# Fewer, longer turns between scoring and weighing in a fused attention and feed-forward kernel

## The chip, the core and the metric

The kernel runs on one core of one Trainium2 chip. The metric is the device time of one execution in microseconds (us); lower is better. Before the change it is 1427.97 us, the median of three runs that lie between 1427.86 and 1428.01 us. Engines are called PE (matrix multiply; PEld are its weight loads), ACT (activation), DVE (vector), POOL (GpSimd) and SP (SyncE, which here issues most of the DMA transfers).

## The reference

The reference is one transformer block without masks, in float32: 2048 tokens, width 512, 32 query heads of width 16 that share one key and one value head, and a gated feed-forward part of width 1792.

```python
q = heads(ln(x) @ wq); k = ln(x) @ wk; v = ln(x) @ wv     # 32 heads of 16; one k, one v
p = softmax(q @ k.T / 4, axis=-1)
h = x + merge(p @ v) @ wo
g = ln(h)
out = h + (gelu(g @ w_gate) * (g @ w_up)) @ w_down
```

## The kernel before

**Blocks and groups.** The queries are cut into four blocks of 512 tokens (NB = 4), the heads into eight groups of four (NG = 8), and the keys into sixteen chunks of 128 (KC = 16). For one group and one block, `score` (L952) is called 32 times, twice for each key chunk. One call is a **pair**: two heads of the group against one chunk. `scores` (L357) runs a pair as two matmuls (L364) on the upper and lower 64 rows of PE at the same time, into one of two PSUM tiles of two banks, and then one exponential of 128x1024 on ACT (L368) into half of a tile `p`. The next pair but one uses the same PSUM tile again, so its matmuls wait until that exponential is done.

**Weighing.** When a chunk's two pairs are through ACT, `weigh` (L370) multiplies `p` with the values, in four matmuls on four column strips of PE (L372), eight in the trace because float32 takes two passes. The sums of a group gather in one bank, `acc`. After the sixteenth chunk `evacuate` (L383) copies `acc` on DVE (L385), sends it to DRAM and fetches it back in another layout (L386, L396), all on SP's queue.

**Cycles.** Scoring uses PE in halves of 64 rows, weighing in strips of 32 columns. The program collects several pairs and then weighs what is finished: that is a **cycle**. `SIZES` (L978) says how many pairs the six cycles of a group have: 6, 5, 5, 6, 5, 5. `finish` (L929) weighs every chunk whose second pair is older than the newest call; at the last cycle of a group (L1093) it weighs all that is left. In a six-cycle group the numbers of weighed chunks are 2, 3, 2, 3, 3, 3.

**Dense work between the pairs.** While attention runs on one block of queries, PE also does the projection and the feed-forward part of the block before (`dense`, L560). That work comes as a generator of **steps**, where one step is two matmuls on the two halves of 64 rows. In the woven part (`weave`, L823) two jobs of twelve steps run side by side, one on each half, and each job changes halves in the middle. After each pair the loop at L1040 draws as many steps as a table of shares says. `WOVEN` (L1030) gives a 6-pair cycle (0, 5, 3, 3, 3, 0), so none after its first pair, five after the second, three after the third, fourth and fifth, and none after the last. A 5-pair cycle gets (0, 5, 3, 3, 0), the last of a group (0, 5, 4, 3, 0) from `LAST` (L1031). That is 73 steps a group. `kinds` (L1032) lays a block's run of dense work over the cycles: four "long" ones and a "gap" for the projection and normalisation, 36 "woven" ones, then four "long" and two "short" ones, which have tables of their own (L1024, L1025). With LEAD (L980) this puts the woven part of each of three blocks from within group 1 to within group 7, and groups 2 to 6 are woven all through.

**Weights.** The gate and up weights of a block are 28 tiles of 512 KB (tile 2f is the gate, 2f + 1 the up part of slice f), in four buffers. `load_w1` (L510) is called for tile i + 4 when the job of tile i is done (L713), so each load stands at that place of SP's queue, and waits there until PE has freed the buffer. Also on SP's queue are the evacuations named above, the next group's queries (`load_q`, L345, two transfers of 200 KB, called at the fifth pair of a group) and the down weights (`load_w2`, L516, 1 MB each). PE, ACT, SP and DVE run these instructions in the order in which the program writes them.

**Gates.** When a gate and an up job are done, DVE and ACT form the gelu. The DVE operations are drawn one after each pair (L1066), and the tanh on ACT (L735) is put at the end of a cycle (`open_gates`, L940) or ahead of the first down job.

Of the kernel before, what the change touches and what calls it, by code (L numbers as in the profile page):

```python
# [48 lines left out]
def kernel(  # L49
# [21 lines left out]
    NB = S // T  # L71
# [3 lines left out]
    NG = H // 4  # L75
    KC = S // P
# [66 lines left out]
    def attend(first):  # L143
        with ExitStack() as outer:
            with tc.manual_schedule(
                engines={mybir.EngineType.PE, mybir.EngineType.Pool, mybir.EngineType.Activation}
            ):
                run(outer, first)


    def run(outer, first):
# [218 lines left out]
        def weigh(acc, p, kc):  # L370
            for j in range(4):
                nc.tensor.matmul(  # L372
                    acc[32 * j : 32 * j + 32, :], v_sb[:, kc, :], p[:, j, :],
                    start=(kc == 0), stop=(kc == KC - 1), skip_group_check=True,
                )
# [3 lines left out]
        def take_out():  # L379
            for step in outs.pop(0):  # L380
                step()
# [541 lines left out]
        PER = NG * KC  # L923
# [3 lines left out]
        pend = []  # L927

        def finish(n):  # L929
            for _ in range(min(n, len(pend))):  # L930
                pb, pg, pkc, pp, pacc, _ = pend.pop(0)
                weigh(pacc, pp, pkc)
                if pkc == KC - 1:
                    evacuate(pb, pg, pacc)
# [5 lines left out]
        def open_gates():  # L940
            while gates:
                gates.pop(0)()
# [9 lines left out]
        def score(n):  # L952

            nonlocal acc
            i, u = divmod(n, 2)
            b, r = divmod(i, PER)
            g, kc = divmod(r, KC)
            if u == 0:
                if kc == 0:
                    cur["qg"] = qgs.pop((b, g))  # L960
                    acc = pss.tile([P, T], F32, tag="acc", bufs=1, name=f"acc_{b}_{g}")
                if kc == 2 and b * NG + g + 1 < NB * NG:
                    key = divmod(b * NG + g + 1, NG)
                    qgs[key] = load_q(*key)
                cur["p"] = sb.tile([P, 4, T], F32, tag="p", bufs=PB, name=f"p_{i}")
            scores(i, cur["p"], cur["qg"], kc, u)
            if u == 1:
                pend.append((b, g, kc, cur["p"], acc, n))
# [6 lines left out]
        width = 1  # L975


        SIZES = (6, 5, 5, 6, 5, 5)  # L978

        LEAD = (3, 2, 2)  # L980
        n, lead = 0, 2 * PER + sum(SIZES[: LEAD[0]])
        with tc.manual_schedule(engines={mybir.EngineType.SP, mybir.EngineType.DVE}):
            parts, said = None, 3
            if first:
# [35 lines left out]
        set_banks("ps_rest")  # L1020
        width = 3

        PLAIN = {5: (0,) * 5, 6: (0,) * 6}
        LONG = {5: (0, 5, 4, 3, 0), 6: (0, 5, 3, 3, 1, 0)}  # L1024
        SHORT = {5: (0, 6, 3, 3, 0), 6: (0, 6, 3, 3, 0, 0)}  # L1025
        assert sum(SIZES) == 2 * KC
        assert [f for fs in RUNS for f in fs] == list(range(FC))
        assert [len(fs) for fs in RUNS] == [4] * (len(RUNS) - 1) + [2]

        WOVEN = {6: (0, 5, 3, 3, 3, 0), 5: (0, 5, 3, 3, 0)}  # L1030
        LAST = (0, 5, 4, 3, 0)  # L1031
        kinds = (  # L1032
            ["long"] * 4 + ["gap"] + ["woven"] * 6 * len(SIZES) + ["long"] * 4 + ["short"] * 2
        )
        todo = list(kinds)
        fixed = ExitStack()
        fixed.enter_context(
            tc.manual_schedule(engines={mybir.EngineType.SP, mybir.EngineType.DVE})
        )
        for c in range(LEAD[0], (NB - 1) * NG * len(SIZES)):  # L1040
            b, cb = divmod(c, NG * len(SIZES))
            if first and (b, cb) in BOUND_STEPS:
                bound_flag(BOUND_STEPS.index((b, cb)))
            cg = cb % len(SIZES)
            size, kind = SIZES[cg], None
            if b > 0 and cb == LEAD[b]:
                assert work is None
                work, todo = dense(b), list(kinds)
            if work is not None:
                kind = todo.pop(0)  # L1050
            if kind == "long":
                shares = LONG[size]
            elif kind == "woven":
                shares = LAST if cg == len(SIZES) - 1 else WOVEN[size]
            elif kind == "short":
                shares = SHORT[size]
            else:
                shares = PLAIN[size]
            due, said = 0, None
            if kind != "woven":  # L1060
                while lazy:
                    lazy.pop(0)()
            for j, share in enumerate(shares):
                score(n)
                n += 1
                if soon or lazy:  # L1066
                    (soon or lazy).pop(0)()  # L1067

                if b > 0 and cb == 1 and j == 3 and outs:
                    take_out()  # L1070

                if kind in (None, "gap") and n % 2 == 0:
                    finish(sum(e[5] < n - 1 for e in pend))
                if kind == "gap" and j == 1:

                    said = next(work)
                due += share
                while due > 0:
                    said = next(work)
                    if said > 0:  # L1080
                        due -= 1
                    elif said == CUT and kind != "short":
                        break

            ends = kind not in (None, "woven") or kind == "woven" and todo[0] != "woven"
            while ends and said not in (CUT, GAP):
                said = next(work)
                assert said < 0, said
            open_gates()
            if work is not None and not todo:  # L1090
                assert next(work, None) is None
                work = None
            finish(sum(e[5] < n - 1 for e in pend) if cg < len(SIZES) - 1 else len(pend))  # L1093
            while behind:
                behind.pop(0)()
            if outs and kind == "woven":
                lazy.extend(outs.pop(0))
            elif outs:
                take_out()
# [261 lines left out]
    def bound_flag(step):  # L1361
        if step == 0:
            nc.gpsimd.dma_start(b2, b_d)
            return
        nc.vector.tensor_reduce(b1, b2, axis=AX.X, op=ALU.max)

        nc.vector.tensor_scalar(flag, b1, (BOUND_MAX / SCALE) ** 2, None, op0=ALU.is_le)
# [69 lines left out]
```

## Time and profile before

| what | value |
|---|---|
| time, median of three runs | 1427.97 us (1427.86 to 1428.01) |
| profiled execution, its own time | 1427.32 us |
| its span, first to last instruction | 1425.5 us |
| granted PE clock, mean | 0.999 |
| instructions in the trace | 25062 |
| mean DMA rate over the span | 127 GB/s |

The profile is one execution. A timeline row gives start and length in us, the engine, the line of the kernel, the operation, output<-inputs by the names in the program, the shape, the number of instructions that the row joins, and in brackets how long the engine had been idle and what ended that. Matmuls overlap, so on PE the distance from one start to the next is what counts, and the length of a row is longer than its share of the time. Rows of SP are the moments of issue of transfers, not the transfers. The windows view gives, for a stretch of time, its length, the busy time and number of instructions of PE, PEld, DVE, ACT and POOL, the granted clock, the busy share of the DMA engines and the rate in GB/s.

### The profile page before, as it was taken

The page shows a single profiled execution, that of the slowest core. Times are in us where ns is not written, and L with a number is a line of the kernel's source. Part 1 is how long each engine was busy: PE and PEld are TensorE (multiplying, and loading weights), DVE is VectorE, ACT ScalarE, POOL GpSimd, SP SyncE. Part 2 cuts the span into 40 slices and gives each one's busy share as a digit, 9 for nine tenths or more (in the row PEclk, how much of TensorE's full clock was granted, in tenths as well). Part 3 has the DMA queues.
Part 4 walks back from the last instruction along what each step waited for, and adds up shares of the span by engine and source line. Part 5 has one row for each costly group of instructions (what it writes and reads, how often), then busy time and mean ns, then how long its engine had stood idle before and what let it go on. Part 6 is the DMA issues. An engine that isn't in the chain of part 4 may idle for free.

```text
span 1425.5 us, 25062 instructions
## 1 busy us (share of the span) xinstructions
PE 1401.7 (98%) x10420; PEld 755.2 (53%) x10420; DVE 544.8 (38%) x985; ACT 1034.3 (73%) x1145; POOL 218.8 (15%) x301
## 2 busy tenths in 40 slices
PE   6999999999999999999999999999999999999998
PEld 5533333224555555555555555554555555557886
DVE  7421322203352433424252432514353342427665
ACT  6699999997777787776877777877777777772000
POOL 5566776731000000000000000000000000000000
PEclk9999999999999999999999999999999999999999
DMA  4456766643242242213252332203343241433551
GB/s 157 145 189 213 230 223 214 214 136 111 83 152 86 93 139 86 86 42 111 94 172 74 102 129 85 87 24 122 101 131 115 87 145 47 138 125 132 176 208 62
DMA packets 66929, 180.56 MB, mean 127 GB/s; under 512 B 9436, under 2 KB 9436, under 8 KB 66776
## 3 DMA queue, kind: packets, MB, share of 16 engines
q1 hardware_dynamic: 56976, 144.79, 30.5%
q0 software_dynamic: 9760, 34.08, 7.3%
q8 instruction: 84, 1.38, 0.4%
q14 instruction: 37, 0.30, 0.1%
q10 hardware_dynamic: 72, 0.00, 0.0%
HBM read 131.13 MB, written 47.71 MB: 125 GB/s over the span
## 4 chain that ended last, share of the span: by engine, by line
PE 91%; ACT 6%; DVE 1%; issue 1%; DMA 0%; SPq 0%; POOL 0%; ACTq 0%; DVEq 0%
PE acc L372 31%; PE s L364 20%; PE pu L858 9%; PE pg L858 7%; ACT p L368 5%; PE pd L858 5%; PE pq L190 4%; PE pd L533 3%; PE pg L555 3%; PE pd L555 3%; PE pu L555 3%; PE pp L533 2%; PE pk L1224 1%; PE pxt L608 1%; PE pt L1214 0%
## 5 line engine op out<-in xcount | busy, mean ns | idle before, releaser
L368 ACT ACTIVATE p<-s 128x1024 f32<-128x1024 f32 x1024 | 965.2, 1059 | 243.1 <-PE s L364 242.4
L372 PE MATMUL acc<-p,v_sb 128*32 128x512 f32 x4096 | 488.2, 598 | 0.1
L364 PE MATMUL s<-qg,kaug 50*128 50x512 f32 x1984 | 395.7, 432 | 4.1 <-ACT p L368 3.3
L364 PEld LDWEIGHTS s<-qg,kaug 50*128 50x128 f32 x1984 | 172.3, 184 | 283.9 <-ACT p L368 164.9
L372 PEld LDWEIGHTS acc<-p,v_sb 128*32 128x32 f32 x4096 | 109.3, 109 | 234.3 <-issue 226.0
L858 PE MATMUL pu<-x2h,w 64*128 64x512 f32 x672 | 211.7, 392 | 0.2 <-DVE g L732 0.2
L858 PE MATMUL pg<-x2h,w 64*128 64x512 f32 x672 | 211.6, 391 | 0.0
L126 POOL TENSOR_SCALAR rstd<-mv 128x1 f32<-128x1 f32 x16 | 3.5, 219 | 984.1 <-DVE mv L124 983.8
L858 PEld LDWEIGHTS pu<-x2h,w 64*128 64x128 f32 x672 | 116.0, 186 | 12.9 <-DVE g L732 0.6
L858 PE MATMUL pg<-x2l,w 64*128 64x512 f32 x336 | 122.6, 392 | 0.0
L858 PEld LDWEIGHTS pg<-x2h,w 64*128 64x128 f32 x672 | 116.3, 186 | 11.1 <-DVE g L732 0.2
L858 PE MATMUL pu<-x2l,w 64*128 64x512 f32 x336 | 122.2, 391 | 0.0
L735 ACT ACTIVATE ga<-ga 128x512 f32<-128x512 f32 x56 | 36.4, 655 | 88.7 <-DVE ga L730 88.7
L858 PE MATMUL pd<-w,gh 64*128 64x512 f32 x384 | 81.4, 391 | 0.0
L385 DVE COPY oT<-acc 128x512 f32<-128x512 f32 x32 | 22.1, 692 | 142.6 <-PE acc L372 142.4
L800 DVE TENSOR_TENSOR h<-h,pd 128x512 f32<-128x512 f32 x48 | 31.9, 685 | 114.5 <-PE pd L858 65.6
L1067 DVE SCALAR_TENSOR_TENSOR ga<-ga,g 128x512 f32<-128x512 f32 x72 | 49.7, 691 | 48.6 <-ACT ga L735 47.1
L401 DVE RECIPROCAL oc<-oc 128x128 f32<-128x128 f32 x64 | 56.3, 922 | 28.8 <-DMA oc<-acc_d 23.7
L719 DVE COPY g<-pg 128x512 f32<-128x512 f32 x56 | 38.7, 692 | 65.8 <-PE pg L858 60.1
L858 PEld LDWEIGHTS pu<-x2l,w 64*128 64x128 f32 x336 | 58.0, 186 | 6.7
L858 PEld LDWEIGHTS pg<-x2l,w 64*128 64x128 f32 x336 | 58.1, 186 | 5.0
L732 DVE TENSOR_TENSOR g<-g,pu 128x512 f32<-128x512 f32 x56 | 38.2, 683 | 40.5 <-PE pu L858 30.2
(251 smaller groups left out, 1387.8 us busy)
## 6 DMA issues: line engine op xcount, KB each, us to landing
w<-w_d SPq DMA_DIRECT2D x112, 512.0 KB
w<-w_d SPq DMA_DIRECT2D x28, 1024.0 KB
qg<-q_d SPq DMA_DIRECT2D x62, 200.0 KB
q_d<-qh SPq DMA_DIRECT2D x32, 256.0 KB
acc_d<-oT SPq DMA_DIRECT2D x32, 256.0 KB
oc<-acc_d SPq DMA_DIRECT2D x128, 64.0 KB
w_d<-w_0b POOLq DMA_DIRECT2D x14, 512.0 KB, 6.6
w_d<-w_1b POOLq DMA_DIRECT2D x14, 512.0 KB, 4.0
```

Of the source, the lines that this page charges most:

```text
L190: nc.tensor.matmul(pq, wt[:, d, c * P : (c + 1) * P], xt[:, d, :], start=(n == 0), stop=(n == 3 * DC - 1),)
L364: nc.tensor.matmul(s[:, a, :], kaug[rows, kc * P : (kc + 1) * P], qg[rows, u, :], start=True, stop=True,)
L368: nc.scalar.activation(p[:, 2 * u : 2 * u + 2, :], s, AF.Exp, scale=SCALE)
L372: nc.tensor.matmul(acc[32 * j : 32 * j + 32, :], v_sb[:, kc, :], p[:, j, :], start=(kc == 0), stop=(kc == KC - 1), skip_group_check=True,)
L401: nc.vector.reciprocal(oc[:, 1, sl], oc[:, 1, sl])
L533: nc.tensor.matmul(banks[k], lhsT[rows], rhs[rows], start=(turn == 0 and i == 0), stop=(turn == 1 and i == n - 1), skip_group_check=True,)
L555: nc.tensor.matmul(bank, lhsT, rhs, start=(i == 0), stop=(i == len(ts) - 1))
L719: nc.vector.tensor_copy(g, pg)
L732: nc.vector.tensor_tensor(g, g, pu, op=ALU.mult)
L735: nc.scalar.activation(a, a, AF.Tanh, scale=GELU_A * GELU_C)
L858: nc.tensor.matmul(e["bank"], lhsT[rows], rhs[rows], start=i == 0 and not e["both"], stop=last and e["both"], skip_group_check=True,)
L1067: (soon or lazy).pop(0)()
```

## The change

Groups 2 to 6 take five cycles of 7, 6, 6, 7 and 6 pairs in place of six. Groups 0, 1 and 7 keep the old sizes. The shares change with them: a 7-pair cycle gets 17 steps, a 6-pair cycle of such a group 13, with two steps in place of three ahead of its last pair. That makes 73 steps a group again, and the chunks weighed in the five cycles are 3, 3, 3, 3 and 4. A block has 43 cycles in place of 48, over three blocks 15 cycles fewer, and the list of kinds has 31 woven entries in place of 36. No matmul, no exponential and no transfer is added or taken away; their order changes.

```diff
-        SIZES = (6, 5, 5, 6, 5, 5)
+        SIXES, FIVES = (6, 5, 5, 6, 5, 5), (7, 6, 6, 7, 6)
+        GROUPS = (SIXES,) * 2 + (FIVES,) * (NG - 3) + (SIXES,)
+        CYCLES = [(g, j) for g in range(NG) for j in range(len(GROUPS[g]))]
...
-        WOVEN = {6: (0, 5, 3, 3, 3, 0), 5: (0, 5, 3, 3, 0)}
-        LAST = (0, 5, 4, 3, 0)
-        kinds = (
-            ["long"] * 4 + ["gap"] + ["woven"] * 6 * len(SIZES) + ["long"] * 4 + ["short"] * 2
-        )
+        WOVEN = {
+            SIXES: {6: (0, 5, 3, 3, 3, 0), 5: (0, 5, 3, 3, 0)},
+            FIVES: {7: (0, 5, 3, 3, 3, 3, 0), 6: (0, 5, 3, 3, 2, 0)},
+        }
+        LAST = {SIXES: (0, 5, 4, 3, 0), FIVES: (0, 5, 3, 3, 2, 0)}
+        woven = len(SIXES) + len(FIVES) * (NG - 3)
+        kinds = ["long"] * 4 + ["gap"] + ["woven"] * woven + ["long"] * 4 + ["short"] * 2
...
-        for c in range(LEAD[0], (NB - 1) * NG * len(SIZES)):
-            b, cb = divmod(c, NG * len(SIZES))
+        for c in range(LEAD[0], (NB - 1) * len(CYCLES)):
+            b, cb = divmod(c, len(CYCLES))
+            group, cg = CYCLES[cb]
+            sizes = GROUPS[group]
...
-            cg = cb % len(SIZES)
-            size, kind = SIZES[cg], None
+            size, kind = sizes[cg], None
...
-                shares = LAST if cg == len(SIZES) - 1 else WOVEN[size]
+                shares = LAST[sizes] if cg == len(sizes) - 1 else WOVEN[sizes][size]
...
-            finish(sum(e[5] < n - 1 for e in pend) if cg < len(SIZES) - 1 else len(pend))
+            finish(sum(e[5] < n - 1 for e in pend) if cg < len(sizes) - 1 else len(pend))
```

More of the change, by code (lines that the diff above doesn't have):

```diff
@@ L975, in run @@
         width = 1
-        SIZES = (6, 5, 5, 6, 5, 5)
+        SIXES, FIVES = (6, 5, 5, 6, 5, 5), (7, 6, 6, 7, 6)
+        GROUPS = (SIXES,) * 2 + (FIVES,) * (NG - 3) + (SIXES,)
+        CYCLES = [(g, j) for g in range(NG) for j in range(len(GROUPS[g]))]
         LEAD = (3, 2, 2)
-        n, lead = 0, 2 * PER + sum(SIZES[: LEAD[0]])
+        n, lead = 0, 2 * PER + sum(SIXES[: LEAD[0]])
         with tc.manual_schedule(engines={mybir.EngineType.SP, mybir.EngineType.DVE}):
@@ L1021, in run @@
         width = 3
-        PLAIN = {5: (0,) * 5, 6: (0,) * 6}
+        PLAIN = {5: (0,) * 5, 6: (0,) * 6, 7: (0,) * 7}
         LONG = {5: (0, 5, 4, 3, 0), 6: (0, 5, 3, 3, 1, 0)}
         SHORT = {5: (0, 6, 3, 3, 0), 6: (0, 6, 3, 3, 0, 0)}
-        assert sum(SIZES) == 2 * KC
+        assert all(sum(sizes) == 2 * KC for sizes in GROUPS)
         assert [f for fs in RUNS for f in fs] == list(range(FC))
         assert [len(fs) for fs in RUNS] == [4] * (len(RUNS) - 1) + [2]
-        WOVEN = {6: (0, 5, 3, 3, 3, 0), 5: (0, 5, 3, 3, 0)}
-        LAST = (0, 5, 4, 3, 0)
-        kinds = (
-            ["long"] * 4 + ["gap"] + ["woven"] * 6 * len(SIZES) + ["long"] * 4 + ["short"] * 2
-        )
+        WOVEN = {
[5 more added lines that the diff above has]
+        kinds = ["long"] * 4 + ["gap"] + ["woven"] * woven + ["long"] * 4 + ["short"] * 2
         todo = list(kinds)
```

## The prediction

> **What bounds the kernel now.** I read the page's busy table first, then its chain of work that ended last, then the timeline of TensorE (PE) for one group of heads whose cycles are all woven, and last the same timeline around two places where cycles were longer than their likes.
>
> ```profile
> PE 1401.7 (98%) x10420; PEld 755.2 (53%) x10420; DVE 544.8 (38%) x985; ACT 1034.3 (73%) x1145; POOL 218.8 (15%) x301
> ...
> PE 91%; ACT 6%; DVE 1%; issue 1%; DMA 0%; SPq 0%; POOL 0%; ACTq 0%; DVEq 0%
> PE acc L372 31%; PE s L364 20%; PE pu L858 9%; PE pg L858 7%; ACT p L368 5%; PE pd L858 5%; PE pq L190 4%; PE pd L533 3%; PE pg L555 3%; PE pd L555 3%; PE pu L555 3%; PE pp L533 2%; PE pk L1224 1%; PE pxt L608 1%; PE pt L1214 0%
> ```
>
> PE carries 91% of the chain, so a change pays only by what it takes from PE's time line. The change leaves every matmul in place: a woven group keeps 32 score pairs, 16 weighings and 73 dense steps. Only the number of turns between scoring and weighing, and what stands between them, can move the time. A cycle starts at the row of four score matmuls, so the differences of these starts are cycle lengths:
>
> ```profile
> 428.43 0.74 PE L364 MATMUL s<-qg,kaug 50*128 50x512 f32 x4
> ...
> 435.21 0.73 PE L364 MATMUL s<-qg,kaug 50*128 50x512 f32 x4
> ...
> 441.91 0.74 PE L364 MATMUL s<-qg,kaug 50*128 50x512 f32 x4
> ...
> 444.57 0.40 PE L364 MATMUL s<-qg,kaug 50*128 50x512 f32 x2
> ...
> 447.69 0.73 PE L364 MATMUL s<-qg,kaug 50*128 50x512 f32 x4
> ...
> 455.32 0.73 PE L364 MATMUL s<-qg,kaug 50*128 50x512 f32 x4
> ...
> 462.00 0.73 PE L364 MATMUL s<-qg,kaug 50*128 50x512 f32 x4
> ...
> 468.87 0.74 PE L364 MATMUL s<-qg,kaug 50*128 50x512 f32 x4
> ```
>
> The six cycles (6, 5, 5, 6, 5, 5 pairs) last 6.78, 6.70, 5.78, 7.63, 6.68 and 6.87 us, 40.44 us together. By the code they weigh 2, 3, 2, 3, 3 and 3 key chunks. The fourth (6 pairs, 14 steps) and the fifth (5 pairs, 11 steps) weigh alike and differ by 0.95 us for a pair and three steps: a pair or a step costs about 0.233 us.
>
> **The change, part by part.** *Cycles.* I price each new cycle from an old one with the same parity of its first pair. Another timeline row gives the price of a weighing, and shows where ScalarE's exponential (ACT) ends the wait:
>
> ```profile
> 608.31 1.92 PE L372 MATMUL acc<-p,v_sb 128*32 128x512 f32 x16
> 610.16 0.73 PE L364 MATMUL s<-qg,kaug 50*128 50x512 f32 x4
> ...
> 614.59 0.49 PE L364 MATMUL s<-qg,kaug 50*128 50x512 f32 x2 [0.15 <-ACT p L368]
> 615.01 2.78 PE L372 MATMUL acc<-p,v_sb 128*32 128x512 f32 x24
> 617.72 0.74 PE L364 MATMUL s<-qg,kaug 50*128 50x512 f32 x4
> ```
>
> Sixteen against 24 matmuls, two against three chunks, are 1.92 against 2.78 us: 0.86 us a chunk. The new group, without waits:
> - first (7 pairs, 17 steps, 3 chunks): 6.78 + 0.93 (a pair, three steps) + 0.86 = 8.57;
> - second and third (6 pairs, 13 steps, 3 chunks): 5.78 + 0.86 + 0.70 (a pair, two steps) = 7.34 each;
> - fourth (7, 17, 3): 5.78 + 0.86 + 2 x 0.93 = 8.50;
> - fifth (6, 13, 4): 6.68 + 0.86 + 0.70 = 8.24.
>
> Sum 39.99, or 0.45 us less than 40.44: the price of one pair of turns.
>
> *What ACT takes back.* The long cycle at 610.16 has 6 pairs, 12 steps, 3 chunks, one step before its last pair, and lasts 7.56 us. The woven 6-pair cycle (7.63 us) less two steps would be 7.16. So the last pair there waits 0.40 us for the exponential that frees its score bank, as the row at 614.59 names. The new 6-pair cycles leave two steps at that place where the old had three. The moment ACT frees the bank stays, so the wait is 0.40 - 0.23 = 0.17 us, three times a group: 0.51. A 7-pair cycle keeps three steps there, and ACT does not fall behind further on:
>
> ```profile
> 448.29 5.61 ACT L368 ACTIVATE p<-s 128x1024 f32<-128x1024 f32 x6 [0.64 <-PE s L364]
> ```
>
> Six of about 1.05 us in 5.61 us start 0.91 us apart, against 0.93 for PE's pair and three steps. Net per group: 39.99 + 0.51 - 40.44 = +0.06, and for 15 groups **+0.9 us**. Bounds: if that wait is nothing, -6.8; if each is the full 0.40, +11. I keep 0.17, since the row beside it differs by one step only.
>
> *Weight loads.* By the instruction order of both kernels, SP issues the same loads; what shifts is how soon after its issue a tile is first used. Two stretches matter, at the start of group 2 in the second and third woven blocks, where the evacuation of the group before holds SP:
>
> ```profile
> 718.80 1.21 SPq L513 DMA_DIRECT2D w<-w_d  x1
> 720.05 0.76 SPq L349 DMA_DIRECT2D qg<-q_d  x2
> 720.86 2.21 SPq L513 DMA_DIRECT2D w<-w_d  x2
> ...
> 1043.67 0.37 SPq L513 DMA_DIRECT2D w<-w_d  x1
> 1044.09 0.76 SPq L349 DMA_DIRECT2D qg<-q_d  x2
> 1044.89 3.12 SPq L513 DMA_DIRECT2D w<-w_d  x2
> ```
>
> The first load is tile 7 (of 28), then come the queries of the next group, then tile 8. What PE did:
>
> ```profile
> 714.02 0.74 PE L364 MATMUL s<-qg,kaug 50*128 50x512 f32 x4
> ...
> 720.80 0.73 PE L364 MATMUL s<-qg,kaug 50*128 50x512 f32 x4
> ...
> 723.14 0.47 PE L858 MATMUL pu<-x2h,w 64*128 64x512 f32 x1
> ...
> 727.88 0.73 PE L364 MATMUL s<-qg,kaug 50*128 50x512 f32 x4
> 728.45 0.39 PE L858 MATMUL pg<-x2h,w 64*128 64x512 f32 x1
> ...
> 1038.91 0.73 PE L364 MATMUL s<-qg,kaug 50*128 50x512 f32 x4
> ...
> 1045.74 0.73 PE L364 MATMUL s<-qg,kaug 50*128 50x512 f32 x4
> ...
> 1048.38 0.47 PE L858 MATMUL pu<-x2h,w 64*128 64x512 f32 x1 [0.23 <-DVE g L732]
> ...
> 1053.12 0.73 PE L364 MATMUL s<-qg,kaug 50*128 50x512 f32 x4
> ```
>
> These second cycles last 7.08 and 7.38 us against 6.70 for their like: PE waited 0.38 and 0.68 us for tile 7, used 4.34 and 4.71 us after its issue. (The view names DVE at 1048.38; the twin at 723.14 has no such release, so I take the load.) In the changed kernel tile 7 is first used at the third step of the second cycle, about 8.57 + 0.57 + 2 x 0.23 = 9.6 us after the group's start; it was there after 9.12 and 9.47. Both waits go: -1.06 us.
>
> Tile 8, used before in the first step of the third cycle (at 728.45, 0.57 us in, and likewise after 1053.12) without a wait, is now used right behind the fourth pair of the second cycle. In the like cycle the fourth pair starts at 444.57 - 441.91 = 2.66, so the use is 8.57 + 2.66 + 0.23 = 11.46 us after the group's start: at 725.48 and 1050.37 on this trace's clock, 4.62 and 5.48 us after issue. Is the tile there? What the queues moved, by the windows view (length, busy columns, DMA share, GB/s):
>
> ```profile
> 720.40:726.60 6.20, 6.20 (x56) 3.71 (x52) 4.34 (x8) 5.48 (x7) 0.00 (x0) 1.00 0.88 235
> 1044.60:1050.65 6.05, 5.82 (x48) 3.44 (x44) 3.85 (x8) 4.99 (x7) 0.00 (x0) 1.00 0.93 239
> 816.51:819.50 2.99, 2.99 (x26) 2.04 (x24) 2.81 (x5) 2.99 (x4) 0.00 (x0) 1.00 0.56 178
> ```
>
> Tile 7, the queries and tile 8 are 512 + 400 + 512 KB, 1.46 MB. At 235 and 239 GB/s that much had moved by 726.60 and 1050.65. The end of a load trails its bytes: at these rates tile 7's 0.52 MB was through about 2.2 us after 720.40 and 1044.60, and PE resumed 0.5 and 1.6 us later. With 1.0 us added, PE gets tile 8 at about 727.6 and 1051.7, and waits 2.1 and 1.3 us. Bounds: nothing, if tile 8 lands 4.3 us after issue as tile 7 did; 3.0 and 3.3 us, since at the first step of the third cycle it was there. I take 3.4 together, from the bytes, which both windows bear out; these cycles then lose their two ACT waits of 0.17: **+3.1 us**.
>
> The row from 816.51 shows an issue to an empty queue, whose half megabyte had moved within 2.99 us. [...]
>
> *Other loads.* Tiles 19 and 27 of the same blocks come closest: from the matmul that frees the buffer to the first use there are 17 pairs and steps, 4.0 us, less about 0.4 for the issue. In the last windows row a load issued at 816.51 to an empty queue had moved its 0.53 MB after 2.99 us. I put 0.1 for all four; with tile 7's 4.34 us it would be 0.7 each. By the same count the first woven block keeps 7 us for its tightest tiles and pays nothing. DVE's and ACT's gate work is one piece a score as before, and I cost its shift at nothing: a 7-pair cycle is 8.5 us long, the longest it now waits for a turn.
>
> Sum against the profiled execution (1427.32 us): +0.9 - 1.06 + 3.1 + 0.1 = **+3.0**, 1430.3. The profiled run lies 0.65 under the median shown, so I forecast **1431.0 us**, just past 0.2% (2.86 us, about what a measurement of this kernel can tell from no change).
>
> **The rivals.**
> 1. *Tile 8 is in time* (not slower). The queries do not hold tile 8, which lands within the 4.6 us it has, as tile 7 did in 4.34. Then +0.9 - 1.06 + 0.1 = -0.1: 1427.9. [...] It decides at one place, the fourth pair of group 2's second cycle. For it: tile 7's times. Against it: only 1.46 MB by 726.60.
> 2. *ACT does not stall the two-step pair* (faster): 15 x -0.45 = -6.8, with +3.4, -1.06 and +0.1: 1423.6. Against it: the row at 614.59.
> 3. *The short-slack tiles wait too* (slower): 4 x 0.7 in place of 0.1: 1433.7. Against it: the empty queue at 816.51.
>
> **How the numbers follow.** Forecast 0.62, of it 0.46 past 2.86 us and 0.16 within, as the sum stands at that edge and its high terms are the less bounded; rival 1 0.20 (0.19 within, 0.01 faster); rival 2 0.05 (0.03 faster, 0.02 within); rival 3 0.13 slower. That makes faster 0.04, within 0.37, slower 0.59. The range runs from just above rival 1, whose spread by 0.03 us on each of 45 ACT waits (1.3 us) half reaches into it, to just above rival 3: 1428.3 to 1434.0.
>
> **What would show it.** Per woven group, five cycles near 8.6, 7.5, 7.5, 8.5 and 8.4 us; rows of the last pair in 6-pair cycles that name ACT; group 2's second cycle 8.5 to 9.3 us in the second and third blocks, with SP's rows unchanged ahead of it. Groups of 40.0 us would prove the ACT wait wrong; a second cycle of 7.5 us there, the load wait.

## The result, and the profile after

The changed kernel takes 1432.58 us (median of 12 runs, 1431.03 to 1434.98), the kernel before 1427.82 us (12 runs, 1426.53 to 1431.88). The ratio is 1.0032, with a 95% interval of 1.0024 to 1.0039: slower by 4.8 us. The profiled execution of the changed kernel took 1433.49 us (span 1431.7 us, mean granted clock 0.998), 6.2 us more than the one of before, so the account below is made for 6.2 us.

The page of the changed kernel, its busy table and its chain of work by engine:

```profile
PE 1403.6 (98%) x10420; PEld 756.4 (53%) x10420; DVE 543.5 (38%) x985; ACT 1031.0 (72%) x1145; POOL 218.3 (15%) x301
...
PE 88%; ACT 6%; DVE 2%; DMA 1%; issue 1%; POOL 0%; SPq 0%; ACTq 0%; DVEq 0%; POOLq 0%
```

PE is busy 1.9 us longer with the same 10420 matmuls. A longer busy time for the same work says that some matmuls took longer; the windows view below shows which. DMA has come into the chain with 1%, and a group row names it:

```profile
L858 PE MATMUL pg<-x2h,w 64*128 64x512 f32 x672 | 213.0, 393 | 3.2 <-DMA w<-w_d 3.2
```

PE was idle for 3.2 us ahead of gate matmuls, until a weight load was there. Now the same timeline as before the change. First one group of five cycles, then where the five woven groups of the first woven block begin and end:

```profile
428.26 0.73 PE L364 MATMUL s<-qg,kaug 50*128 50x512 f32 x4
...
436.88 0.73 PE L364 MATMUL s<-qg,kaug 50*128 50x512 f32 x4
...
444.40 0.73 PE L364 MATMUL s<-qg,kaug 50*128 50x512 f32 x4
...
451.91 0.74 PE L364 MATMUL s<-qg,kaug 50*128 50x512 f32 x4
...
460.42 0.74 PE L364 MATMUL s<-qg,kaug 50*128 50x512 f32 x4
...
468.84 0.73 PE L364 MATMUL s<-qg,kaug 50*128 50x512 f32 x4
```

```profile
387.70 0.74 PE L364 MATMUL s<-qg,kaug 50*128 50x512 f32 x4
...
590.61 0.73 PE L364 MATMUL s<-qg,kaug 50*128 50x512 f32 x4
```

The same two places in the kernel before:

```profile
387.96 0.73 PE L364 MATMUL s<-qg,kaug 50*128 50x512 f32 x4
...
590.34 0.74 PE L364 MATMUL s<-qg,kaug 50*128 50x512 f32 x4
```

The cycles are 8.62, 7.52, 7.51, 8.51 and 8.42 us, 40.58 in all. Five groups take 202.91 us against 202.38, which is 0.11 us a group more. So the saved turn is not seen at all. The rest of the loss lies in four cycles of the second and third woven blocks. Two of them hold the wait for tile 8. PE, then SP's queue:

```profile
722.80 0.73 PE L364 MATMUL s<-qg,kaug 50*128 50x512 f32 x4
...
728.26 0.46 PE L858 MATMUL pg<-x2h,w 64*128 64x512 f32 x1 [2.38 <-DMA w<-w_d]
...
734.34 0.74 PE L364 MATMUL s<-qg,kaug 50*128 50x512 f32 x4
...
1052.50 0.73 PE L364 MATMUL s<-qg,kaug 50*128 50x512 f32 x4
...
1056.41 0.46 PE L858 MATMUL pg<-x2h,w 64*128 64x512 f32 x1 [0.83 <-DMA w<-w_d]
...
1060.95 0.73 PE L364 MATMUL s<-qg,kaug 50*128 50x512 f32 x4
```

```profile
720.45 0.77 SPq L349 DMA_DIRECT2D qg<-q_d  x2
721.26 3.13 SPq L513 DMA_DIRECT2D w<-w_d  x2
...
1049.09 0.76 SPq L349 DMA_DIRECT2D qg<-q_d  x2
1049.89 4.19 SPq L513 DMA_DIRECT2D w<-w_d  x2
```

These cycles last 11.54 and 8.45 us against 7.51: 4.03 and 0.94 more. Tile 8 is issued right behind the queries at 721.26 and 1049.89, and PE gets it 7.0 and 6.5 us later. But an idle time of 2.38 us alone does not make a cycle 4 us longer. The windows view of that stretch (length; busy time of PE, PEld, DVE, ACT and POOL; granted clock; DMA share; GB/s) shows the rest:

```profile
728.00:729.00 1.00, 0.74 (x6) 0.74 (x8) 0.00 (x0) 0.00 (x0) 0.00 (x0) 0.93 1.02 414
729.00:730.00 1.00, 1.00 (x6) 0.89 (x6) 0.00 (x0) 0.12 (x1) 0.00 (x0) 0.50 1.04 426
730.00:731.00 1.00, 1.00 (x6) 0.38 (x2) 0.00 (x0) 0.91 (x1) 0.00 (x0) 0.50 1.03 426
731.00:732.00 1.00, 1.00 (x10) 0.29 (x12) 0.00 (x0) 0.78 (x1) 0.00 (x0) 0.50 0.21 82
732.00:733.00 1.00, 1.00 (x16) 0.28 (x12) 0.20 (x1) 0.77 (x2) 0.00 (x0) 0.86 0.00 0
```

About 0.6 us after PE resumes, its granted clock falls to 0.50 and stays there for 3.4 us (0.14 us of the first row, three whole rows, 0.28 us of the last). Pairs and steps start 0.43 us apart there (at 729.17, 729.60, 730.02 and 730.45 us), where the prediction has 0.233. 3.4 us at half the clock are an estimated 1.7 us of work less, and 4.03 less the 2.38 of idle time leave 1.65: about 1.6 us of the 4.03 are this.

The other two long cycles are the first of group 5 in these blocks. ACT, then PE:

```profile
840.60 3.77 ACT L368 ACTIVATE p<-s 128x1024 f32<-128x1024 f32 x4 [2.84 <-PE s L364]
844.24 0.65 ACT L735 ACTIVATE ga<-ga 128x512 f32<-128x512 f32 x1
844.76 2.88 ACT L368 ACTIVATE p<-s 128x1024 f32<-128x1024 f32 x3
```

```profile
839.97 0.73 PE L364 MATMUL s<-qg,kaug 50*128 50x512 f32 x4
...
845.86 0.49 PE L364 MATMUL s<-qg,kaug 50*128 50x512 f32 x2 [0.16 <-ACT p L368]
...
849.00 0.74 PE L364 MATMUL s<-qg,kaug 50*128 50x512 f32 x4
```

A tanh (line 735) stands between the fourth and the fifth exponential, in mid-cycle, and the last pair waits for ACT: 9.03 us in place of 8.60. The tanh stood there before the change too. ACT in the kernel before, in the same cycle of the same block:

```profile
836.42 3.78 ACT L368 ACTIVATE p<-s 128x1024 f32<-128x1024 f32 x4 [2.17 <-PE s L364]
840.06 0.66 ACT L735 ACTIVATE ga<-ga 128x512 f32<-128x512 f32 x1
840.58 1.96 ACT L368 ACTIVATE p<-s 128x1024 f32<-128x1024 f32 x2
```

That cycle had six pairs and lasted 6.8 us, as others of its kind did. Its sixth and last pair needs the score bank that the fourth exponential frees, ahead of the tanh. The changed cycle has a seventh pair, which needs the bank of the fifth, behind it. The third block shows the same (1166.62 to 1175.65). Where the tanh stands behind the fifth exponential, as in group 3's first cycle (at 763.99), the cycle lasts 8.60 us and loses nothing.

**The account.** Groups 3 x 0.53 = 1.6; tile 8 4.03 + 0.94 = 5.0, about 1.6 of it the clock; the tanh 2 x 0.43 = 0.85; tile 27 in the second block 0.2 (the cycle from 904.56 lasts 8.75 us against 8.54 for its likes, and PE resumes 3.7 us after the tile's issue); the waits of before for tile 7, which are gone, -1.06. Sum 6.6. Measured from the start of group 2 to the start of group 7, the three blocks are 0.53, 4.80 and 1.15 us longer, 6.5 together; outside these groups the changed execution is 0.3 us shorter, which makes the 6.2. Without the clock's fall the terms come to 5.0 us, near the median's 4.8; whether every execution has that fall is taken up in the last section.

### The profile page after: what moved, and what is told of

It reads as the page before. It is cut to its first block, busy times and chain, and to the rows that moved or that the text cites. A ratio compares the mean times of both kernels' runs of the same rounds, so it can differ in the third digit from the quotient of the medians.

```text
span 1431.7 us, 25046 instructions
## 1 busy us (share of the span) xinstructions
PE 1403.6 (98%) x10420; PEld 756.4 (53%) x10420; DVE 543.5 (38%) x985; ACT 1031.0 (72%) x1145; POOL 218.3 (15%) x301
## 4 chain that ended last, share of the span: by engine, by line
PE 88%; ACT 6%; DVE 2%; DMA 1%; issue 1%; POOL 0%; SPq 0%; ACTq 0%; DVEq 0%; POOLq 0%
PE acc L372 30%; PE s L364 19%; PE pu L858 8%; PE pg L858 7%; ACT p L368 6%; PE pd L858 5%; PE pq L190 3%; PE pd L533 3%; PE pg L555 3%; PE pd L555 3%; PE pu L555 3%; PE pp L533 2%; DMA w<-w_d 1%; PE pxt L608 1%; PE pk L1230 0%
```

## The experiments

In what follows theory T is the prediction's, corrected by the trace after: ACT eats what the turn saves, the queue holds tile 8, PE's idle time halves the clock, and the tanh ahead of the exponential that a seventh pair needs costs 0.85 us. Each run's time is a median, with the ratio to the kernel before on the same chip.

**Does the queue hold tile 8, and what in it?** Two moves, each in both kernels. The first puts the queries behind tile 8: `load_q` is called at the group's 13th pair in place of its fifth.

```diff
-                if kc == 2 and b * NG + g + 1 < NB * NG:
+                if kc == (6 if n > lead else 2) and b * NG + g + 1 < NB * NG:
```

> The changed kernel, with the load of the next group's queries called at the ninth... that is, one pair earlier than the group's eighth key chunk instead of the third, so that these two transfers stand behind tile 8 on SP's queue and no longer ahead of it. Theory T (the queries and the late tile 7 ahead of it hold tile 8, and the clock halves because PE then idles): group 2's second cycles in the second and third woven blocks come down from 11.54 and 8.46 us to about 7.5, the stretch of granted clock 0.50 near 729 us goes with them, the span loses 4 to 5 us, about 1428 us. Rival R1 (the queries do not matter; it is the evacuation's wait ahead of tile 7, or the sheer rate of the queue): the wait for tile 8 stays at 1 to 2.4 us, the time at 1431 to 1433 us.

1430.04 us (1.0016, 1.0007 to 1.0025). PE and SP in that place:

```profile
723.06 0.74 PE L364 MATMUL s<-qg,kaug 50*128 50x512 f32 x4
...
730.58 0.74 PE L364 MATMUL s<-qg,kaug 50*128 50x512 f32 x4
```

```profile
720.80 3.83 SPq L513 DMA_DIRECT2D w<-w_d  x3
...
725.16 0.80 SPq L349 DMA_DIRECT2D qg<-q_d  x2
```

The cycle lasts 7.52 us, its twin in the third block too, and the clock stays whole: the queries ahead of tile 8 made the wait, and the wait made the clock fall. Rival R1 is out. The long cycles of the woven part are 5.4 us shorter in all. The median fell by only 2.5, to 2 us above the 1428 that theory T expected, which these cycles do not explain.

> The kernel before, with the queries' load called at the later key chunk as in the first kernel of this call. Tile 7 stands ahead of the queries anyway and tile 8 was in time, so theory T expects no change: within 0.5 us of 1427.8. If the queries' move is itself worth microseconds in any kernel, this one shows it, and the gain of the changed kernel with the same move has to be read less by that.

1429.34 us (1.0010, 1.0001 to 1.0019): 1.8 us more, where theory T expected nothing, and no cycle of the woven part is longer than before. So this move has a cost of its own, somewhere else. The second move takes the evacuation's wait out of tile 7's way, by calling the fetch of the sums one cycle later:

```diff
-            if b == 0 and g < NG - 1:
+            if b > 0 and 1 <= g < NG - 2:
+                outs.extend([[], [turn_out]])
+            elif b == 0 and g < NG - 1:
                 outs.append([turn_out])
```

> The changed kernel, with the second half of an evacuation (the transfers that fetch the sums back, whose wait holds SP's queue) called one cycle later for groups 1 to 5 of the blocks after the first; tile 7, the queries and tile 8 are then issued without that wait ahead of them. Theory T: SP issues tile 7 some 3 to 4 us sooner, tile 8 follows as soon as its buffer is free, and the wait for tile 8 and the halved clock go: about 1428 us. Rival R1 in the form that the queries' place alone matters: tile 8 still stands behind the queries, the wait stays, 1431 to 1433 us. If the later fetch makes the projection of that group late, a new wait shows in the next cycles.

1429.98 us (1.0015, 1.0006 to 1.0024). The long cycles come down to 8.04 and 7.52 us; a wait of 0.44 us for tile 8 is left in the first, as the queries are still ahead of it. The time again lies 2 us above theory T's. Either move is nearly enough for tile 8: what decides is how much stands between the free buffer and tile 8's bytes.

> The kernel before, with the same move of the fetch by one cycle. Theory T: the two waits for tile 7 (0.38 and 0.68 us) go, nothing else changes: about 1 us less than before, 1426.8 us. Rival (those two waits were not the load's but the gate's on DVE, which the view named at one of them): no change, 1427.8 us, with second cycles of 7.08 and 7.38 us as they were.

1426.58 us (0.9991, 0.9982 to 1.0000). The two second cycles last 6.69 and 6.68 us in place of 7.08 and 7.38: both waits were the load's, and the view that named DVE at 1048.38 misled. The move shifts some of DVE's work too, but not the operation that the view named: in the third block it starts 1.92 us into the cycle in the kernel before and 1.93 us with the move, and with the move the matmul starts at 1047.48, ahead of that operation's end at 1048.07.

**Is it ACT that eats the turn?** Both kernels with a quarter of the exponentials of groups 2 to 6 left out, in the blocks after the first (`w` is 384 there and 512 elsewhere):

```diff
-            nc.scalar.activation(p[:, 2 * u : 2 * u + 2, :], s, AF.Exp, scale=SCALE)
+            nc.scalar.activation(
+                p[:, 2 * u : 2 * u + 2, :w], s[:, :, :w], AF.Exp, scale=SCALE
+            )
+            if w < T:
+                nc.gpsimd.memset(p[:, 2 * u : 2 * u + 2, w:], 1.0)
```

> The changed kernel with a lighter ACT: in groups 2 to 6 of the blocks after the first, each exponential covers 384 of the 512 columns of each head, and POOL sets the other 128 columns to 1; a quarter of the exponentials there is left out. Theory T (ACT's exponential ends the wait ahead of the last pair of a 6-pair cycle with two steps there): the second and third cycles of a group come down from 7.51 to 7.34 us and the fifth from 8.43 to 8.24, a group from 40.6 to 39.9 to 40.1 us; group 2's long second cycle in the second and third woven blocks stays long, since PE comes to tile 8 even sooner. Rival R2 (the extra 0.17 us are a cost of PE's own, of the steps or of the turn, and not a wait for ACT): the cycles stay at 7.51 and 8.43 us and the group at 40.6.

> The kernel before with the same lighter ACT (the same quarter of the exponentials left out). Theory T: six cycles have almost no wait for ACT, a group goes from 40.44 to no less than 40.2 us; five cycles of the lighter kernel are then 0.3 to 0.45 us a group shorter than six, the price of one pair of turns, where with the full exponentials they are 0.1 longer. Rival R2: both kinds of group change alike or not at all, and five cycles stay the longer ones.

1423.41 us (0.9974, 0.9964 to 0.9984) and 1424.55 us (0.9976, 0.9965 to 0.9987). One group of five cycles with the lighter ACT:

```profile
427.31 0.73 PE L365 MATMUL s<-qg,kaug 50*128 50x512 f32 x4
...
435.78 0.74 PE L365 MATMUL s<-qg,kaug 50*128 50x512 f32 x4
...
443.12 0.73 PE L365 MATMUL s<-qg,kaug 50*128 50x512 f32 x4
...
450.48 0.73 PE L365 MATMUL s<-qg,kaug 50*128 50x512 f32 x4
...
458.99 0.74 PE L365 MATMUL s<-qg,kaug 50*128 50x512 f32 x4
...
467.22 0.73 PE L365 MATMUL s<-qg,kaug 50*128 50x512 f32 x4
```

And of six, first and last row:

```profile
427.96 0.73 PE L365 MATMUL s<-qg,kaug 50*128 50x512 f32 x4
...
468.17 0.74 PE L365 MATMUL s<-qg,kaug 50*128 50x512 f32 x4
```

The five cycles are 8.47, 7.34, 7.36, 8.51 and 8.23 us: the prediction's lengths without waits, within 0.1 us. Five take 39.91 us, six 40.21. So with a lighter ACT a saved turn does pay, 0.30 us a group; with the full exponentials five take 40.58 and six 40.44. Rival R2 is out. Six cycles also lose 0.23 us when ACT gets lighter: they had small waits for ACT too, of 0.05 to 0.08 us in four of the six cycles, which the prediction had taken for none.

**Where must the steps stand?** One more deal of the same 13 steps, on top of the kernel with all three moves (below):

```diff
-            FIVES: {7: (0, 5, 3, 3, 3, 3, 0), 6: (0, 5, 3, 3, 2, 0)},
+            FIVES: {7: (0, 5, 3, 3, 3, 3, 0), 6: (0, 4, 3, 3, 3, 0)},
...
-        LAST = {SIXES: (0, 5, 4, 3, 0), FIVES: (0, 5, 3, 3, 2, 0)}
+        LAST = {SIXES: (0, 5, 4, 3, 0), FIVES: (0, 4, 3, 3, 3, 0)}
```

> The changed kernel with the three moves and the drains, and with the steps of the 6-pair cycles of groups 2 to 6 dealt 0, 4, 3, 3, 3, 0 in place of 0, 5, 3, 3, 2, 0: 13 steps as before, but three of them ahead of the last pair. Theory T (ACT runs its exponentials back to back from the first pair on, about 0.93 us each, and the last pair can't start before the fourth of them is done, wherever the steps stand): the second, third and fifth cycles stay at 7.5, 7.5 and 8.4 us, 1427.2 us as with the old deal. Rival R5 (it is the place with two steps that makes the wait): the cycles go to 7.34, 7.34 and 8.24 us, 1419 to 1421 us.

1429.84 us (1.0017, 1.0008 to 1.0027), 2.6 us more than theory T expected. The cycles get no shorter; they last 7.57, 7.58 and 8.50 us. So R5 is out: it is not the place with two steps that makes the wait. But theory T's "wherever the steps stand" does not hold either. With four steps ahead of it, the third pair comes before the first exponential is done, and the wait has moved there (its row at 438.67 us starts 0.36 us behind the last step, where the changed kernel's at 438.60 starts 0.22 behind); each of the three cycles is 0.06 us longer than with the old deal, 2.7 us over 45 cycles, which is the miss. In both deals a 6-pair cycle of 13 steps has about 0.17 us too little work for PE while ACT works off the first exponentials.

**The tanh in mid-cycle.** Where its gate is already there, it goes to the end of a cycle:

```diff
-                        assert not gates and not lazy or all(j // 2 in gs for j in fs)
-                        open_gates()
+                        if not all(j // 2 in gs for j in fs):
+                            open_gates()
```

> The changed kernel, with the tanh of the gates not put ahead of the first down job where its gate is already there; it then goes to the end of a cycle. Theory T (the tanh in mid-cycle sits on ACT ahead of the last exponentials of group 5's first cycle in the second and third woven blocks): these two cycles go from 9.02 to about 8.60 us, 0.85 us in all, the long waits for tile 8 stay, about 1431.7 us. Rival R3 (these cycles wait for a down weight or for DVE): they stay at 9.0 us and the time at 1432.6.

1432.16 us (1.0031, 1.0018 to 1.0043). In the second block, and the wait for tile 8 in the same run:

```profile
838.11 0.73 PE L364 MATMUL s<-qg,kaug 50*128 50x512 f32 x4
...
846.72 0.73 PE L364 MATMUL s<-qg,kaug 50*128 50x512 f32 x4
```

```profile
727.95 0.46 PE L858 MATMUL pg<-x2h,w 64*128 64x512 f32 x1 [2.10 <-DMA w<-w_d]
```

Group 5's first cycles last 8.61 and 8.60 us: the 0.85 us were the tanh, and R3 is out. The cycles show it, not the median, which is 0.4 us lower where the run's own times spread over 3.5 us. By chance this run says something on the clock as well: here PE was idle for 2.10 us, the clock stayed at 1.00, and the cycle took 9.70 us in place of 11.54.

**What the moves cost at the end.** In the kernels with a move the time from the last addition on DVE (line 800 or 802) to the end of the span was longer: 6.2 and 6.3 us in the two kernels without a move, but 8.2 and 8.3 with the late queries (before and changed), 7.4 and 8.0 with the late fetch. SP's waits for itself from 1400 us on, in the changed kernel with late queries (us in total, times, longest):

```profile
SPq L1408 <- SPq L1408: 5.1, 2, 3.0
```

and of the kernel with all three moves and twelve drains:

```profile
SPq L1412 <- SPq L1412: 3.0, 1, 3.0
```

The first wait of 3.0 us is for the last stores. The second, 2.1 us, falls between two closing instructions, and the profile names nothing but SP itself as its end. The moves change how many waits SP's stream holds (733 instructions of SP in the trace without a move, 739 to 748 with one), and instructions come by DMA, on two queues of their own in the page of the changed kernel with late queries (packets, MB, share; the rows do not say for which engines):

```profile
q8 instruction: 84, 1.38, 0.4%
q14 instruction: 39, 0.32, 0.1%
```

That is 16 KB a packet on the first and 8 KB on the second. Theory P says that the closing instructions then lie across the border of two fetches of 8 KB. Drains (`nc.sync.drain()`) shift them. The program has them behind the last store, but in the traces they run from 16 to 22 us into the span, at places 36 to 50 of SP's stream (to 66 where there are 28). All that they change near the end is thus the place of the closing instructions:

```diff
     attend(True)
+    for _ in range(12):
+        nc.sync.drain()
```

> The kernel before, with twelve drains on SP behind its last store and nothing else. Theory P (in both kernels with a move of the first call that stood still at the end, SP waited for its own closing instructions, because these lay across the border of two fetches of 8 KB; twelve places more put them there in this kernel too): everything up to the last matmul stays, SP stands still for 1 to 2 us among its closing instructions, 1428.6 to 1429.6 us. Rival (that stand belonged to the moved loads): no change, 1427.6 us.

1429.23 us (1.0016, 1.0007 to 1.0025): 8.2 us from the last addition to the end. The drains alone, in the kernel before, bring the pause about, though not all of it in one place: 0.9 us lie ahead of the first closing wait and 1.0 us among the last ones.

> The kernel before with the fetch of the sums one cycle later, and 28 drains on SP behind its last store, which put the closing instructions past the border. Theory P: the stand of about 1 us at the end of the same kernel without the drains goes, and the two waits for tile 7 stay away: 1425.4 to 1425.9 us. Rival: 1426.6 us as without the drains.

1425.65 us (0.9988, 0.9979 to 0.9997). The last addition of this kernel, and its span:

```profile
1417.93 0.69 DVE L802 TENSOR_TENSOR hp<-hp,pd 128x512 f32<-128x512 f32 x1 [0.67 <-PE pd L557]
```

```profile
span 1424.2 us, 25073 instructions
```

6.3 us again, where the same kernel without drains has 7.4. Twelve drains bring the pause into the kernel before, twenty-eight take it out of the one with the late fetch: it is a matter of place, as theory P says. That the fetch itself is what SP waits for is argued, from its size and its time. This version, six cycles with the late fetch and the drains, is 1.7 us under the kernel before, by an interval that just excludes no change, and has the lowest median of the kernels that do the whole work.

**All three moves together**, with twelve drains:

> The changed kernel with the three moves together (the queries' load later, the fetch of the sums one cycle later, the tanh at the end of the cycle), and with twelve drains on SP behind its last store, which shift SP's closing instructions in their stream by 12 places (in the two kernels of the first call SP had stood still for 1.8 and 2.1 us among those closing instructions, which the two kernels without the moves do not do). Theory T: no load wait and no tanh wait is left, five cycles take 40.5 to 40.6 us a group against 40.44, the two waits for tile 7 are gone; 1427.0 to 1428.3 us, no difference from before. Rival (five cycles cost in themselves more than the group times show): 1430 us or more; or, if a turn does pay when its waits are gone: 1424 us.

1427.23 us (0.9997, 0.9988 to 1.0006): no difference from the kernel before. No load wait and no tanh wait is left, and a group takes 40.6 us. Five cycles, without their side effects, are worth nothing here. Next to six cycles with the late fetch and the drains (0.9988) they come out some 1.3 us longer; the intervals overlap, but 15 groups at 0.11 us more would make 1.6.

**Filling ACT's wait with work.** On top of the three moves and the drains, the third step is given back to the 6-pair cycles in two of the three blocks:

```diff
+        FULL = (0, 5, 3, 3, 3, 0)
...
+                if b in full and size == 6 and sizes is FIVES and todo[0] == "woven":
+                    shares = FULL
```

> The changed kernel with the three moves and the drains, and with the third dense step given back ahead of the last pair of the 6-pair cycles in the first two of the three blocks: 76 steps a group in place of 73, so that the woven part ends one cycle sooner and one cycle of the next block has no dense work. Theory T: the 0.17 us waits for ACT are filled (14 or 15 steps a block, 0.17 us each: 2.4 us), a group takes about 40.8 us with 76 steps; the cycle without dense work waits for ACT for about 1.2 us; 1.3 us a block less, 1424.7 us. Rival R4 (the steps come faster than SP's loads, or the plain cycle costs as much as the filled waits): 1427 us or more.

1431.99 us (1.0034, 1.0021 to 1.0046): a miss. The 6-pair cycles do 14 steps in 7.58 us against 13 in 7.51, so the wait is filled as theory T says. But most of it is gone again when the next block begins with a cycle more that has no dense work (the first block is 0.4 us shorter in all), and in the second block a down job waits for DVE:

```profile
843.23 0.79 PE L860 MATMUL pd<-w,gh 64*128 64x512 f32 x2 [2.38 <-DVE g L734]
```

```profile
844.00:845.00 1.00, 1.00 (x8) 0.81 (x6) 0.00 (x0) 0.51 (x1) 0.00 (x0) 0.50 0.74 98
```

PE is idle for 2.38 us, and the clock halves again: that cycle takes 12.75 us. DVE is busy for 0.90 us of the 1.00 from 842.00 us on and for 0.24 of the next, and the multiplication that the row names (line 734) comes behind three operations on the fetched sums (lines 404 to 416). That PE wants the bank of the up sums, which line 734 reads, is argued from the code. Rival R4's time came true, its reasons only in part: no matmul waits for a load, and the wait for DVE stood in no expectation.

## Why the prediction was right, and where it was not

- *What bounds the kernel, and the cycles without waits.* Right. The lengths without ACT's waits (8.57, 7.34, 7.34, 8.50, 8.24) are those of the lighter ACT within 0.1 us.
- *What ACT takes back.* Right in mechanism: 7.51 to 7.52 us where 7.51 was forecast, and 8.42 where 8.41 was. The group came to +0.11 us and not +0.06 against before, 1.6 us in place of 0.9 for 15 groups. The sum had taken the six cycles of before to be free of waits for ACT. They held 0.23 us of them, so the saved turns are worth 0.30 us, not 0.45, and ACT takes 0.67 us back from five cycles (40.58 against 39.91) and 0.23 from six, 0.44 more where the prediction had 0.51. That the net came out near is in part luck: 0.15 less saved and 0.07 less taken back have opposite signs.
- *Tile 7.* Right: both waits are gone, and the runs with the late fetch show that they were the load's.
- *Tile 8: the mis-sized term.* Foreseen were waits of 2.1 and 1.3 us, 3.4 in all, and +3.1 for the sum. PE was idle for 2.38 and 0.83 us, 3.2 in all. The reckoning by bytes was thus good in sum, with one wait 0.3 us too short and the other 0.5 too long. But in the profiled execution the two cycles lost 5.0 us, since the prediction priced a wait at its length, and the first wait was followed by 3.4 us at half the clock.
- *The gates, costed at nothing: the step that failed.* The prediction costed the gates by how long one waits for a turn. But this tanh kept its place in mid-cycle, behind the fourth exponential; what is new is a seventh pair that needs the fifth, and it cost 0.85 us in two places. The 8.5 us that I named as the cover are a bound on how long a gate waits, not on what waits behind it on ACT.
- *Other loads.* 0.1 forecast, 0.2 measured, all at tile 27.
- *Rival 1* fell: tile 8 was not there in 4.6 us. The trace has 7.0 and 6.5 us from issue to use, behind the tile and the queries ahead; without the queries ahead, in the run with late queries, the wait was gone. *Rival 2* fell with the group of 40.58 us. *Rival 3* (1433.7) came nearer to the time than the forecast, but not by its mechanism: tiles 19 and 27 hardly waited.

The forecast, 1431.0 us, lies 1.6 us under the median, and its direction was right. Against the profiled execution the sum missed 3.2 us: 1.6 for the clock, 0.85 for the tanh and 0.7 for the groups, all of the same sign. Against the medians it missed 1.8, about what the tanh and the groups make without the clock.

## What to carry to other kernels

Before one counts the turns that a longer cycle saves, one should ask which engine paces the cycle when they are gone: here ACT needed 0.91 us a pair, and each of the three 6-pair cycles had a step too few to cover it. A shift of work against a queue is to be read at the first use of each transfer, with all that stands ahead of it in the queue; and a wait of PE can cost more than its length, as here 2.38 us of waiting made a cycle 4.03 us longer. A difference of 1 to 2 us can come from a pause of SP at the program's end (here up to 8.3 us from the last addition to the end, in place of 6.2), so two kernels should be compared up to the last matmul as well as in the whole.

## What the runs showed that I had not expected

**The clock fell after 2.3 us without work.** PE's idle times for a load or for DVE, and the clock after them: 2.38 us (tile 8, changed kernel), 2.34 us (tile 8, third block, with the lighter ACT) and 2.38 us (DVE, filled cycles) each brought 3.4 us at 0.50; 2.10, 1.53, 1.15, 0.83 and 0.44 us did not. By the clock records it is not the length alone: behind the last matmul the clock fell after 2.06 us in the changed kernel with the late fetch, and only after 4.65 us in the kernel before. In the changed kernel the record of the full clock begins at 22.30 us, and the clock falls at 728.86, rises at 732.27 and falls at 1428.59: 207, 1 and 204 times 3.413 us. In the kernel before it begins at 24.42 and falls at 1423.89 us, 410 times as much. So in these two traces the clock changed only on a grid of 3.41 us. In the three cases above 62 to 70% of the 3.41 us ahead of the fall were idle; the 1.53 us can take 45% of such an interval at most. Where the 2.10 us lay on the grid is not shown; that they fell across the border of two intervals is argued, not shown.

The ends of the programs agree. Behind the last matmuls the 3.41 us ahead of the fall were idle for about 60% (changed, late fetch), 71% (before, late fetch), 86% (before, late queries), 95% (changed) and 100% (before, before with drains, changed with late queries). In the last three the interval ahead of that one was idle for 34 to 36%, and no fall followed it. By these numbers, a run in which the same idle time falls otherwise on the grid would be an estimated 1.6 us shorter. The changed kernel's times fit: the five longest (1433.5 to 1435.0 us) have a mean granted clock of 0.998, the seven others (1431.0 to 1432.9) 0.999, and 3.4 us at half the clock are 0.0012 of the span. But the mean also moves with the fall at the program's end, so that the clock makes this spread is argued, not shown.

**SP paused for 1 to 2 us among its closing instructions**, by where they lie in their stream, as the drains show: 8.2 us from the last addition to the end with twelve drains in the kernel before, 6.2 without. Five of the kernels here have that pause (7.4 to 8.3 us), each by an edit that lies more than a hundred of SP's instructions ahead of the end.
